# GpSimd adds two shifted score patterns in bf16 for 26 of 160 VectorE key groups of a fused attention and ReGLU kernel

## The chip, the cores and the metric

The kernel runs on one core of a Trainium2 chip. The metric is the device time of one execution, in microseconds. The time before is 677.84 us, the median of three runs (676.66 to 677.92).

Six engines matter here. TensorE multiplies matrices (PE in the profile, with its weight loads shown as PEld), ScalarE (ACT) evaluates exponentials, VectorE (DVE) and GpSimd (POOL) do elementwise work, SyncE (SP) issues most DMAs. Each engine executes its own list of instructions in order, and waits on semaphores that the others raise. [...]

## The reference

With x of 2048 rows and 512 columns, the result is x plus an attention block plus a gated feed-forward block, both fed by the same layer norm. Attention has 32 heads of 16 columns, the feed-forward block 1792 hidden columns:

```python
        scores = jnp.einsum("bhqd,bhkd->bhqk", q, k) * (Dh ** -0.5)
        p = _softmax(scores, axis=-1)
        o = jnp.einsum("bhqk,bhkd->bhqd", p, v)
...
        gate = gate * (lambda x, dt: x.astype(dt))(gate > 0, gate.dtype)
        h = gate * up
        return jnp.einsum("bsf,fd->bsd", h, W_down)
...
    xn = _layernorm(x, axis=-1)
    return x + _A_ref(xn, A_wqkv, A_wo) + _B_ref(xn, B_W_gate, B_W_up, B_W_down)
```

## The kernel before

Attention is the bulk. Its work is cut into 512 key groups: four blocks of 512 queries, four groups of eight heads, the even or the odd four heads of such a group, and sixteen tiles of 128 keys. One key group has four score tiles of 128 keys by 512 queries, one for each head. A score tile is one step of TensorE with four matmuls (`score`, L1584), and half of the array works on it. The softmax needs no maximum here, so a group only needs exp of its scores, and then the product with the values ("pv" steps, `pv_stream`, L1540); a column of ones beside the values gives the sum for the division.

Exponentials are made in two ways:

- 352 groups go to ScalarE. Each is two units (704 in all), and one unit is an exp over 128x1024 scores from PSUM into a slot of `ring` (L1654). Two PSUM slots alternate between units.
- 160 groups go to VectorE and GpSimd (`quad`, L1607; `QUADS` says how many in each of the 32 blocks). VectorE turns each of the four score tiles into 16-bit integers with one add and a clamp at zero (L1615, named d1). Read as bf16, such an integer is a rough exponential: the exponent bits are right, and the fraction is a straight line. To smooth the line, three such patterns are summed: the raw one, and two more that have the integers 31 and 81 added (`SHIFTS`, L433). Before the change GpSimd makes the two shifted patterns from the raw one with a 64-bit integer add over four packed lanes (L1629, named p3, one instruction of 128x2048 16-bit numbers for each pattern). VectorE makes them (L1632) in the first two and the last two groups only. TensorE then does the sum itself: it runs the product with the values once for each of the three patterns, and all of them accumulate in the same PSUM bank. So such a group has six pv steps, two halves of the array for each of the three tensors.

Raw patterns have four buffers (`NRAW`), shifted ones five (`NPAT`). The projections, the gated feed-forward block and the output rows are cut into jobs of a few TensorE steps each and threaded between the units.

GpSimd's instructions come from two sets. `load_library` (L1018) issues one small 64-bit add whose only use is to bring in the set that holds it, with `LIB_NS = 7000` as its cost in the plan. The operations that carry the name "stock", which are the power of the layer norm (L929, a `tensor_tensor`) and the last `iota` (L1667), belong to the other set: the small add is ordered behind those that exist by then, and the iota behind every p3. The kernel has no instruction that loads a set by name.

The order of all instructions was planned beforehand and is written out as a list of operation numbers, `ORDER`, with the buffer numbers in `SLOTS`. `Graph.follow` (L543) replays it: each engine's queue is the list restricted to that engine. It also makes each GpSimd operation that is marked `port` wait for the last VectorE operation so marked before it in the list.

Of the kernel before, what the change touches and what calls it, by code (L numbers as in the profile page):

```python
# [81 lines left out]
POOL_NS = 1014  # L82
LIB_NS = 7000
# [657 lines left out]
def bass_parallel_sum__mha_block__glu_gated_reglu__prompt_kernel(  # L741
# [13 lines left out]
    with ExitStack() as es:  # L755
# [44 lines left out]
        P_b = Pool("b", 4)  # L800
        P_ring = Pool("ring", NRING)
        P_raw = Pool("raw", NRAW)
        P_pat = Pool("pat", NPAT)
        P_qf = Pool("qf", 2)
        P_xn = Pool("xn", 4)
        P_q = Pool("q", NQ)
# [903 lines left out]
```

## Time and profile before

| view | figure |
|---|---|
| median of three runs | 677.84 us |
| profiled execution, its own time | 680.3 us |
| profiled execution, span from first to last instruction | 678.5 us |
| TensorE clock granted, mean | 1.000 |
| GpSimd busy | 334.1 us, 345 instructions |
| ScalarE busy | 659.1 us |
| DMA, mean over the span | 42 GB/s |

The span is shorter than the execution's own time by 1.8 us, which lie around the first and the last instruction. [...] Idle time is put down to what ended it; "issue" stands where the engine waited for nothing that the profile shows.

### The profile page before, as it was taken

Reading aid. Unit: us, or ns where it says so; the run is one execution under the profiler, and the core shown is the slowest. Engines: PE = TensorE matmul, PEld = TensorE weight load, DVE = VectorE, ACT = ScalarE, POOL = GpSimd, SP = SyncE. Lnnn points to the kernel's source line nnn. Section 1 sums busy time; section 2 is a strip of 40 time slices with the busy share of each in tenths; the row PEclk is TensorE's granted clock in tenths of the full one; section 3 lists DMA queues with packets and bytes.
Section 4 is the critical chain, followed back from the end, with each engine's and each line's share of the span. In section 5 each row is a group of like instructions: output and inputs, shape, how many; then the busy total and the mean of one; then the engine's idle time right before and its main releaser. Section 6 shows DMA issues by size and latency. Waiting matters only on the chain.

```text
span 678.5 us, 46119 instructions
## 1 busy us (share of the span) xinstructions
PE 667.7 (98%) x22348; PEld 394.5 (58%) x20912; DVE 594.7 (88%) x1001; ACT 659.1 (97%) x721; POOL 334.1 (49%) x345
## 2 busy tenths in 40 slices
PE   8999999999999999999999999999999999999997
PEld 3455566565565766665665655555565555555663
DVE  8958999998998888999999787999999777889886
ACT  7999999999999999999999999999999999999995
POOL 3201554654546645555556535654546642535650
PEclk9999999999999999999999999999999999999999
DMA  6420111131411121110101110020200012020101
GB/s 195 58 71 13 43 32 27 24 95 40 118 38 28 37 57 29 27 54 19 38 7 26 36 42 22 23 74 4 59 7 19 22 44 72 23 80 15 31 4 43
DMA packets 51478, 28.77 MB, mean 42 GB/s; under 512 B 18840, under 2 KB 50328, under 8 KB 51288
## 3 DMA queue, kind: packets, MB, share of 16 engines
q1 hardware_dynamic: 51144, 25.70, 14.6%
q8 instruction: 169, 2.77, 1.7%
q14 instruction: 21, 0.17, 0.1%
q10 hardware_dynamic: 144, 0.13, 0.1%
HBM read 18.22 MB, written 2.10 MB: 30 GB/s over the span
## 4 chain that ended last, share of the span: by engine, by line
PE 95%; DVE 2%; ACT 1%; issue 1%; DMA 0%; SPq 0%; POOL 0%
PE ps L481 95%; ACT ring L1654 1%; DVE stats L945 0%; DMA x_sb<-in_A_x_dram 0%; DVE xn_sb L968 0%; SPq L858 0%; DVE xnT L1013 0%; DVE o_sb L1410 0%; DVE up_sb L1412 0%; DVE qf L1414 0%; ACT up_sb L937 0%; DVE o_sb L1407 0%; ACT up_sb L936 0%; POOL rstd L943 0%; ACT xn_sb L1429 0%
## 5 line engine op out<-in xcount | busy, mean ns | idle before, releaser
L1654 ACT ACTIVATE ring<-ps 128x1024 bf16<-128x1024 f32 x704 | 651.1, 1085 | 7.4 <-PE ps L481 6.5
L481 PE MATMUL ps<-qT,kT 64*32 64x512 bf16 x8192 | 470.5, 375 | 1.8 <-issue 0.7
L1615 DVE TENSOR_SCALAR qd<-ps 128x512 int16<-128x512 f32 x640 | 418.8, 685 | 53.4 <-PE ps L481 47.3
L1629 POOL INT64_ADD qd<-qd x312 | 321.0, 1043 | 282.0 <-PE ps L481 132.6
L481 PE MATMUL ps<-qd,v_aug 64*32 64x512 bf16 x3840 | 297.1, 375 | 0.5 <-issue 0.4
L1595 PEld LDWEIGHTS <-kT 64*32 64x32 bf16 x8156 | 178.9, 92 | 113.6 <-issue 26.6
L481 PE MATMUL ps<-ring,v_aug 64*32 64x512 bf16 x2816 | 241.6, 375 | 0.4 <-issue 0.2
L1567 PEld LDWEIGHTS <-v_aug 64*32 64x32 bf16 x5256 | 129.5, 92 | 61.2 <-issue 11.8
L481 PE MATMUL ps<-xnT,wgs 64*32 64x512 bf16 x1792 | 136.7, 375 | 0.6 <-issue 0.6
L481 PE MATMUL ps<-xnT,wus 64*32 64x512 bf16 x1792 | 135.9, 375 | 0.0
L481 PE MATMUL ps<-Wd,hT 64*32 64x512 bf16 x768 | 60.9, 375 | 0.0
L1048 PEld LDWEIGHTS <-wus 64*32 64x32 bf16 x1792 | 45.2, 92 | 22.4 <-issue 2.9
L1048 PEld LDWEIGHTS <-wgs 64*32 64x32 bf16 x1792 | 44.2, 92 | 22.4 <-issue 3.5
L1048 PEld LDWEIGHTS <-hT 64*32 64x32 bf16 x1792 | 44.5, 92 | 21.4 <-issue 2.7
L481 PE MATMUL ps<-Wv,hT 64*32 64x512 bf16 x512 | 44.2, 375 | 0.4 <-issue 0.4
L481 PE MATMUL ps<-Wk,hT 64*32 64x512 bf16 x512 | 43.8, 375 | 0.0
L1269 DVE SCALAR_TENSOR_TENSOR hT<-ps,up_sb 128x512 bf16<-128x512 f32 x56 | 38.5, 687 | 5.5 <-PE ps L481 4.8
L1265 DVE COPY up_sb<-ps 128x512 f32<-128x512 f32 x56 | 38.4, 686 | 3.0 <-PE ps L481 2.1
L481 PE MATMUL ps<-Wo_p,x_sb 64*32 64x512 bf16 x480 | 40.5, 375 | 0.1
L481 PE MATMUL ps<-xnT,Wq 64*32 64x512 bf16 x480 | 36.8, 375 | 0.0
L481 PE MATMUL ps<-xnT,Wk 64*32 64x512 bf16 x480 | 35.6, 375 | 0.9 <-DVE xnT L1013 0.8
L481 PE MATMUL ps<-Wv,xnT 64*32 64x512 bf16 x512 | 31.6, 375 | 0.5 <-DVE kT L1106 0.4
(81 smaller groups left out, 219.6 us busy)
## 6 DMA issues: line engine op xcount, KB each, us to landing
wus<-in_B_W_up_dram SPq DMA_DIRECT2D x38, 128.0 KB, 2.9
wgs<-in_B_W_gate_dram SPq DMA_DIRECT2D x38, 128.0 KB, 2.7
xr_sb<-in_A_x_dram SPq DMA_DIRECT2D x16, 128.0 KB, 2.3
qT<-qf SPq DMA_DIRECT2D x120, 16.0 KB, 2.6
o_sb<-o_sb SPq DMA_DIRECT2D x60, 32.0 KB, 2.4
out_dram<-xn_sb SPq DMA_DIRECT2D x15, 128.0 KB, 2.1
x_sb<-in_A_x_dram SPq DMA_DIRECT2D x8, 128.0 KB, 2.8
Wd<-in_B_W_down_dram SPq DMA_DIRECT2D x6, 128.0 KB, 2.8
```

What stands on the lines that cost most here:

```text
L481: return e.add_instruction(mybir.InstMatmult(name=e.bass.get_next_instruction_name(), engine=mybir.EngineType.PE, ins=[e.lower_ap(x), e.lo ...
L1048: e.ldweights(w()[rows, 32 * j:32 * j + 32], tile_position=(rows.start, 32 * j))
L1265: G.op("DVE", 603, lambda e: e.tensor_copy(up_sb[:, tup.slot, :], bank_of(tu)), reads=[tu], writes=[tup], prio=-590)
L1269: G.op("DVE", 603, lambda e: e.scalar_tensor_tensor(out=hT[:, th.slot, :], in0=bank_of(tg), scalar=0.0, in1=up_sb[:, tup.slot, :], op0=ALU ...
L1567: e.ldweights(vs(j), tile_position=(64 * half, 32 * j))
L1595: e.ldweights(ks(m), tile_position=(64 * half, 32 * m))
L1615: G.op("DVE", 601, lambda e, j=j, tx=tx: e.tensor_scalar(qd[:, tq.slot, 512 * j:512 * j + 512], ps[:, BANK[tx.slot], :], IBIAS[3], 0.0, op ...
L1629: G.op("POOL", POOL_NS, lambda e, x=x, n=n: e.int64_add(x().bitcast(I64), raw().bitcast(I64), SHIFTS[n + 1] * LANES), reads=[ti, tq, t_lib ...
L1654: exp_ops[u] = G.op("ACT", ACT_NS, lambda e, tr=tr, k0=k0: e.activation(ring[:, tr.slot, :, :], ps[:, 4 * k0:4 * k0 + 2, :], ACTF.Exp, sca ...
```

## The change

Of the 160 VectorE groups, numbered from 0, every fifth from number 10 to number 135 is treated differently, 26 in all. In such a group GpSimd makes the first shifted pattern as before (p3). Then, for each of the four quarters, it makes the second shifted pattern of that quarter in a small buffer `cuts` (named p5, an integer add of 128x512 16-bit numbers) and adds it in bf16 to the same quarter of the first pattern, in place (named p4, a `tensor_tensor`). There is one buffer `cuts`. TensorE then multiplies two tensors with the values, the raw one and the sum, in four pv steps where there were six. The groups, units, buffers and all constants of the plan stay as they were.

```diff
+ADD_NS = 1130
+CUT_NS = 290
+ADD_PRIO = 3
+ADD_SHARE = 0.2
+ADD_OFF = 0.0
+FIRSTA = 8
+LASTA = 24
...
+        cuts = sb("cuts", [128, 1, 512], I16)
...
+        P_cut = Pool("cut", 1)
...
-                kinds[bk + (t,)] = KINDS[len(kinds) % len(KINDS)]
+                kinds[bk + (t,)] = 3
+        for i, k in enumerate(kinds):
+            if FIRSTA <= i < len(kinds) - LASTA and int(i * ADD_SHARE + ADD_OFF) > int((i - 1) * ADD_SHARE + ADD_OFF):
+                kinds[k] = 2
...
+        def added(key, u, ti, tq, raw, ta, xa):
+
+            G.op("POOL", POOL_NS, lambda e: e.int64_add(xa().bitcast(I64), raw().bitcast(I64), SHIFTS[1] * LANES),
+                 reads=[ti, tq, t_lib], writes=[ta], prio=u, name="p3", port=True)
+            sums = []
+            for j in range(4):
+                cut = slice(512 * j, 512 * j + 512)
+                tc = Tile("cut", P_cut)
+                c = lambda tc=tc: cuts[:, tc.slot, :]
+                G.op("POOL", CUT_NS, lambda e, cut=cut, c=c: e.int64_add(c().bitcast(I64), raw()[:, cut].bitcast(I64), SHIFTS[2] * LANES),
+                     reads=[ti, tq, t_lib], writes=[tc], prio=u + ADD_PRIO, name="p5", port=True)
+                sums.append(G.op("POOL", ADD_NS, lambda e, cut=cut, c=c: e.tensor_tensor(xa()[:, cut].bitcast(BF16), xa()[:, cut].bitcast(BF16), c().bitcast(BF16), ALU.add),
+                                 reads=[ta, tc], prio=u + ADD_PRIO, name="p4", port=True))
+            ta.w += sums
+            for t, x, more in ((ti, raw, [tq]), (ta, xa, [])):
+                pv_stream(key[:3], key[3], [(lambda rows, j=j, x=x: x()[rows, 512 * j:512 * j + 512].bitcast(BF16)) for j in range(4)],
+                          [t] + more, u, u + PV_LAG, "DVE")
...
+            nq[0] += 1
+            if kinds[key] == 2:
+                added(key, u, ti, tq, raw, ta, xa)
+                return prev
             tb, xb = made("qb")
-            nq[0] += 1
...
-        added = [o for o in G.ops if o.name == "p3"]
+        patterns = [o for o in G.ops if o.name in ("p3", "p4")]
...
-        G.op("POOL", LIB_NS, lambda e: e.iota(pid, pattern=[[0, 2]], base=0, channel_multiplier=1), reads=t_masks, writes=[t_pid], prio=NU, order=added + t_rbz.w, name="stock")
+        G.op("POOL", LIB_NS, lambda e: e.iota(pid, pattern=[[0, 2]], base=0, channel_multiplier=1), reads=t_masks, writes=[t_pid], prio=NU, order=patterns + t_rbz.w, name="stock")
```

`ORDER` and `SLOTS` are replaced as a whole: each changed group has 21 operations instead of 16, so the numbers shift, and the list grows from 8030 to 8160 entries. The plan is a fresh one, which the few words with the change call "not searched". The first changed group has the numbers 1206 (p3), then 1207, 1209, 1211, 1213 (p5) and 1208, 1210, 1212, 1214 (p4). Its GpSimd part of the list, with what stands between left out, reads

```
1207 p5, 1208 p4, 1209 p5, 1210 p4, 1260 p3, 1211 p5, 1261 p3, 1212 p4, 1213 p5, 1292 p3, 1214 p4
```

where 1260, 1261 and 1292 are patterns of the groups behind it. All 26 have this form: the p5 and the p4 alternate, and up to two of the other groups' p3 lie between some of them.

More of the change, by code (lines that the diff above doesn't have):

```diff
@@ L92 @@
     91, 92, 101, 102, 112, 115, 94, 103, 118, 113, 95, 340, 341, 116, 119, 104, 96, 122, 117, 342, 120, 343, 105, 344, 121, 98, 123, 100, 345, 124, 365,
[312 rows of a table removed]
[317 rows of a table added]
 ]
 SLOTS = [int(c, 36) for c in (
-    "0001213130200012110232110324115016720118009101a13b210c30210d311ef011012011103220313450108210913670012cd011a0b001e10f001130012110231453080190"
-    "11611703c1d03001a1b001e0f32031110201320030142815008191300611720c112d0001a90241b201021e00f0021312a10112134201312411508321230901261073203c1122"
-    "3db0121ab00030e100f1300211301021c40123101421115300819300216202700312cdd43010a32103b0301e3f002103201001220031e4315003180239026f204313270021c3"
@@ L410 @@
-    "21d0a123b00021e0f2134130211011002201133014101g503011218309231622070112304cd320a1131b0311ehf2030110132130123131021040315024018139020601220071"
-    "i3cd003a0102303b103204e3f0101j30120022310302140351020813920361272030120c1d0131ab042010312ef0130101100131212303402135103040118139011022670121"
-    "c3121d0a2112b01224311e0302f1103311002213302103435008031090020161201344720013cd002130a0b021ef300003513002311232013004124350200118390031162010"
-    "67011c0d0013a0112b031170ef01100431013001213030113423500083110194611071c0311d002a11201b31210121230e21124f02041125011310010118109036111730124c"
@@ L414 @@
-    "13d10311a0103b3032013320e013120f0431005100312310821191403130602137001cd0100142301a303b0210233001e314f0014103125000010120018290016217002c102d"
-    "03010314a2b00212230e21f32040112500011001018001921204300116021003712cd320213a30b00121231021e21340101f1034115300021302120328110961701304031c21"
-    "3d52031ab03123231103300e1113f0401142030503101000301341809301611371420c113d030a1310b012311301e2f130215100411300502010101000811096061120104310"
-    "70c11010d0a2311b7021023200e124021f041226850110021000128301209002611130070140c11d0091a1b3310213131300e0311224f001145c010103001300381901030211"
@@ L418 @@
-    "067010c10dd0a3013b40300012313011231ef001302013450200231214g0318903021000631207032c1d0302a12h1b002321300372e100f403014503000c110d01a10b101200"
-    "11410081103903060170021030010e1012f123004315000304c10d3001a3b1031031001102018394210201617201123031200100e110f011402150010c1d1001a110b0101030"
-    "180110401922161710312220333124e213020f1302405c1d32130a113b0331001208301034020936213702203120302e0120f00013432140520011cd01011330a1103b101100"
-    "031812300190360104730221131003431ef0010101450113103cd01420a310b300501100100213830900326130722312122730e0310f200412005031c001d3192a3b02001031"
@@ L422 @@
-    "014302018a39001604207300222311320111ebf2100401200523c1211d000001210ab0103011041010211820e960122702120133f100e11f0011402402050c012023d0a11gb0"
-    "1030110101080193306h01312047012310103012e31f0i4011305110c10d310013ab010310j423010100118900116700231312132032e11f023112402140050c3112d03a3211"
-    "21b1031200133482013902261003742321300032100e01f202140051202001412c1d00a213b31020810090160730010320203013e1f401411315203101103310c11d1101a000"
-    "12b1012819332013164170321310e011f01411540011210c0311112d021101ab120821012900617230022130032e1314023f001450200001030010c31d20022a1b0081231113"
@@ L426 @@
-    "4900301670300221240303130e11f2104015000103130011c1300003d0a11301b002831090010166750201313001e3104231f04731015300310130c0013d0010a3180b203801"
-    "934032106200317200212130290021e30f0421350020011200c0123401d00a1b420208012009617001123113103e11001f031203134130151010310c16d301431a1b01821291"
-    "026117210202112301e231f1021140015013401010001131c0032d14ab01830911376702130100110123")]
+    "0001213130200012110232110324115061702180101090213a11b0c12d0e13f1030011011022021330314150281190613700c121d0a011b00e1f001310021113024135018019"
@@ new lines @@
+    "0116117030c13d00a11b200e13f0301110210030234018250180119030461102701c102d001a1922b001e201f002013a1201211323014241115038022019310206310272031c"
+    "123d10b2a13b0001e0410f30020111301211c2310241113500813090262310702043c12d03d0a2130b003e0130f02001311020002212300e413010350038129340f261070100"
+    "c12d3001a103b2000e113f320103131010120104330004310g5000181139100361001170023c112d03a1013hb0001e100f0113010110102213243030241050313801390i0062"
+    "13070200c31d0031a1230jb00e1022f00002401013012010330103412530202813009036100734012c0211d002a011b020e10f01000101011000221013201024112351008129"
@@ new lines @@
+    "00206104731002c10d10201a1212b021e1103f0001103010310213301300401050134841009100601017030113c13d500a123b000e1123f30101461100211300014031115073"
+    "800129016112071000c101d00230a1103b0210e01421f02001101102002011132040130510428100930230611702200c103d202a3312b0034e11123f02201333001243125033"
+    "0212013402813900061201071032c100d201a10211b000e411f002010133001140151001101110038211900363117203c0114d3041a0113b01e110f101210310142101502230"
+    "0311100028112090146010070c11100d301a10b102e101f004213030241005013002101002800101902060111027033c110d0301a11023b0204e113f03102111323033415003"
@@ new lines @@
+    "101013028211920306215170c31241d030a1133b0020e01013f021201323000043100503012401002081229100063130703c51d2003a11020b03e10f30000421120330104110"
+    "52030011112000381219200610171000021c160d201a11000b310e00412f00021623070243110250001010102181180920316100127013c4112d0001a102b003e2113f092321"
+    "13433020431250223021003101812019102611c173032c10014d20a102b0032de011f023121133300104210504131001031110g381019120301006300017001033c11d03ah14"
+    "120b0030e11f0327111031034113501301c134d10003012311103a011b0322181390031613171043e110f001211302143103510c011d2010214211000a1210b0801901006101"
@@ new lines @@
+    "07031e01010f03211121033003141353013c411d000010110a1122b01380119026110701110e121f042211130021410250c021d02320133012303a012b100281129020361427"
+    "032e00103f021212330131421115002c1014d2033001013000a01032b202008139100336010070012e13f20330201234040122500013c1d103053011210013a1024b20100811"
+    "90060112700e71200f0002201213024119235030c112d000201110410a1010b01a028122930106112703e1013f00102b132301004133520041c1200d1012011311022a100331"
+    "b00381940103601272023ee2111f022211030343311f35002c11d003000110010g1a1124b00108012091002612070210e1hf1023021143000421153002ci110d201001011101"
@@ new lines @@
+    "2a011b02j1801090100306130704002e132f000221130230032413050302c1131d002401100a130b030048139000613037023e10001f3032121330414101510a1310b203c103"
+    "1d010311431011819100610710120e11f0000121133000410225020a10b20c1200d0101131000483110910036013237003e13f04021103300414050a210b20210c120d002010"
+    "1102081122900136217103e011f00412310330241115301a1130b022c132d23003001113018114390023611170031e123f002201300204311330502a110b02011c10024d0001"
+    "1212101180210902261072306e1510f000201230042174050311a10b000c0102d0382011132108131390103061227401e311f109132021213034213135030a113b0141c13d01"
@@ L431 @@
+    "1031221103381139001601171040e11f002210301302400152200a1132b000c12d6002401210028119200161272011e12313f002211303413520a11b03c4101d010170210810"
+    "90061703e01f0010110123")]
 LOG2E = 1.4426950408889634
```

629 rows, old and new, of the table ORDER are left out of this document.

## The prediction

> **What bounds the kernel now.** I read the page's table of engines first, then the chain of work that ended last, then the costliest groups.
>
> ```profile
> span 678.5 us, 46119 instructions
> ...
> PE 667.7 (98%) x22348; PEld 394.5 (58%) x20912; DVE 594.7 (88%) x1001; ACT 659.1 (97%) x721; POOL 334.1 (49%) x345
> ...
> PE 95%; DVE 2%; ACT 1%; issue 1%; DMA 0%; SPq 0%; POOL 0%
> ...
> L1654 ACT ACTIVATE ring<-ps 128x1024 bf16<-128x1024 f32 x704 | 651.1, 1085 | 7.4 <-PE ps L481 6.5
> ...
> L1629 POOL INT64_ADD qd<-qd x312 | 321.0, 1043 | 282.0 <-PE ps L481 132.6
> L481 PE MATMUL ps<-qd,v_aug 64*32 64x512 bf16 x3840 | 297.1, 375 | 0.5 <-issue 0.4
> ```
>
> TensorE and ScalarE are both full. The chain lies on TensorE for 95% of the span, yet ScalarE's 704 exps occupy 651.1 us and leave it only 7.4 us idle, 6.5 of them behind TensorE. Less TensorE work can therefore bring at most about 7 us, unless the exps shrink too, and they do not. GpSimd is the engine with room: half idle, nothing of it on the chain, and the products that read its patterns (`ps<-qd,v_aug`) stood idle for 0.5 us in all.
>
> Next I cut the span at the first instruction of GpSimd for what will be the first changed group and after the last one for the last changed group, in the windows view, with the rows of the timeline that give the two edges.
>
> ```profile
> 0.00:96.91 96.91, 93.07 (x2858) 51.59 (x2762) 80.25 (x165) 92.11 (x107) 28.98 (x46) 1.00 0.29 72
> 96.91:572.09 475.18, 472.87 (x16072) 286.17 (x14988) 425.23 (x690) 470.41 (x511) 259.82 (x254) 1.00 0.15 39
> 572.09:678.50 106.41, 101.72 (x3446) 56.71 (x3166) 89.25 (x148) 96.60 (x106) 45.34 (x46) 1.00 0.12 31
> ```
> ```profile
> 96.91 2.06 POOL L1629 INT64_ADD qd<-qd  x2 [1.23 <-DVE qd L1615]
> ...
> 567.99 4.10 POOL L1629 INT64_ADD qd<-qd  x4 [8.02 <-DVE x_sb L1534]
> ```
>
> The columns are busy time and count of TensorE, its weight loads, VectorE, ScalarE and GpSimd, then the granted clock (1.00 throughout). The changed groups lie in the middle 475.2 us; 203.3 us lie outside.
>
> **What GpSimd pays when the kind of instruction changes.** This decides the case. These are the rows of GpSimd's groups with shapes, and its timeline at three places.
>
> ```profile
> L929 POOL TENSOR_TENSOR rstd<-vare,expo 128x1 f32<-128x1 f32 x7 | 3.8, 558 | 4.6 <-DVE vare L927 4.6
> L929 POOL TENSOR_TENSOR rstd<-vare,expo 128x4 f32<-128x4 f32 x2 | 2.5, 1230 | 0.2
> L835 POOL MEMSET rb<- 128x512 f32 x2 | 1.1, 528 | 21.6 <-DVE qd L1632 21.6
> L839 POOL CAST identf<-ident 128x128 f32<-128x128 bf16 x1 | 0.3, 293 | 0.0
> L840 POOL CAST selp<-ident 128x4 f32<-128x4 bf16 x1 | 0.2, 189 | 0.0
> L1021 POOL INT64_ADD ints<-ints x1 | 0.2, 183 | 5.4 <-issue 5.4
> L1667 POOL IOTA ints<- 128x2 int32 x1 | 0.1, 129 | 6.9 <-issue 6.9
> ```
> ```profile
> 6.62 0.65 POOL L943 TENSOR_TENSOR rstd<-vare,expo 128x1 f32<-128x1 f32 x1 [0.23 <-DVE vare L939]
> ...
> 26.75 1.41 POOL L929 TENSOR_TENSOR rstd<-vare,expo 128x4 f32<-128x4 f32 x1
> 33.52 0.18 POOL L1021 INT64_ADD ints<-ints  x1 [5.36 <-issue]
> ...
> 63.01 1.04 POOL L1629 INT64_ADD qd<-qd  x1 [7.16 <-DVE qd L1615]
> 64.01 0.29 POOL L839 CAST identf<-ident 128x128 f32<-128x128 bf16 x1
> 67.49 2.06 POOL L1629 INT64_ADD qd<-qd  x2 [3.19 <-DVE qd L1615]
> 69.48 0.53 POOL L835 MEMSET rb<- 128x512 f32 x1
> 69.98 1.04 POOL L1629 INT64_ADD qd<-qd  x1
> ```
> ```profile
> 658.01 2.05 POOL L1629 INT64_ADD qd<-qd  x2 [2.25 <-PE ps L481]
> 667.00 0.13 POOL L1667 IOTA ints<- 128x2 int32 x1 [6.94 <-issue]
> ```
>
> A cast or a memset follows an integer add, and the reverse, with no gap (63.01, 64.01; 69.48, 69.98). But the first integer add behind the `tensor_tensor` of L929 comes 5.36 us late, and the `iota` behind the last integer add 6.94 us late, both with nothing to wait for. I read them as two swaps of GpSimd's instruction set, one in each direction. The code says which operations are on which side: L929's power, a `tensor_tensor`, and the `iota` are named "stock", and the set of the integer adds is loaded only behind the former. The ten `tensor_tensor` of the trace, nine of L929 and the one at 6.62, all run ahead of the first swap (the last of them at 26.75). The new p4 is a `tensor_tensor`, and it stands between integer adds.
>
> [...]
>
> **The change part by part.**
>
> TensorE: 26 groups lose two pv steps of four matmuls each, 208 of 22348. At 667.7 us / 22348 = 29.9 ns a matmul that is 6.2 us; by the middle window, 472.9 us / 16072 = 29.4 ns, it is 6.1. Take 6; at the other end nothing, where ScalarE sets the pace. VectorE and ScalarE keep their instructions, and so does the DMA queue.
>
> GpSimd: each changed group loses one p3 and gains four p5 and four p4. A p3 costs 1.03 us (two in 2.06). The p5 is not in the trace: between 0.18 us (L1021, one word) and 1.04 us (four times the size); on the line between them, 512 numbers being 128 words of 64 bits, 0.18 + 127/511 x 0.86 = 0.39 us; I take 0.40. The p4's work of 512 bf16 is bounded by 0.53 us (a memset of 512, which reads nothing) and 1.23 us (L929's power of four numbers). The casts give (293 - 189) / 124 = 0.84 ns a number; two inputs at that rate, 0.19 + 2 x 0.43 = 1.05 us; take 1.1. So 104 pairs are 104 x 1.5 = 156 us, between 74 and 236.
>
> Swaps: in the order list a p5 stands ahead of each of the 104 p4 and a p3 or p5 behind it, because there is one buffer `cuts`. None of the p4 are neighbours. So each p4 brings one swap in and one out, 208 in all, beside the two of before. One of each is 5.36 + 6.94 = 12.30 us; 104 x 12.30 = 1279 us. If all were as the shorter row, 1115; as the longer, 1444.
>
> Who waits: both pv halves of the sum need all four p4, and TensorE's queue is in order, so everything behind them stands: the next scores, hence ScalarE's next exp and VectorE's next d1. In the order list 8 to 16 exps (mean 10) stand between a group's first p5 and its last p4, 10 x 651.1 / 704 = 9.3 us of planned cover, and one or two more ahead of the first pv of the sum. Seven swaps (43 us) now lie inside that stretch and the eighth behind it, before the next p3.
>
> The sum is bounded by two paths.
>
> Path A, GpSimd alone sets the middle. 286 p3 remain; by the list 16 lie ahead of the first changed group and 40 behind the last p4, so 230 are inside: 237 us. With 1279 + 156 that is 1672 us, and with the 203.3 outside 1875 us.
>
> Path B, no swap hides behind anything and GpSimd's extra arithmetic hides in its idle half: 678.5 + 1279 - 6 = 1952 us.
>
> Which is nearer? When the first pv of the sum blocks TensorE, the list has already given VectorE the d1 of about three further groups (four raw buffers), so GpSimd has p3 work as soon as it returns; and while it swaps back and does them (5.36 + some 5 us), TensorE runs the five to eight us up to the next changed group's d1. GpSimd then hardly waits. I take A and 15 us of waits: a span of 1890, and with the 1.8 us between this execution's span and its own 680.3 us a time of 1892. The median shown, 677.84, is 2.5 us below the profiled execution, which is nothing at this size.
>
> The low end is A with the cheapest of everything, 203 + 1115 + 74 + 237 = 1629, or 1631 as a time. The high end is B with the longer swap, 678.5 + 1444 - 6 = 2116; the dearest p4 and p5 would add up to 236 - 156 = 80 if nothing covered them, of which I take some and stop at 2150.
>
> [...]
>
> **The rivals.**
>
> R1, one direction is cheap: only the return to the integer adds costs, 104 x 5.36 = 557 us. Path A gives 203 + 557 + 156 + 237 = 1153, path B 1230; about 1195. For it: the kernel starts with stock operations and shows no such gap. Against it: the `iota` returns to operations used before, and its row is the longer of the two.
>
> R2, the other side: no swap, because a plain bf16 add of `tensor_tensor` is among the operations that stay, as cast and memset do; only the power would be stock. Then GpSimd has 334 + 156 - 27 = 463 us of work, still under its span, and TensorE's 6 us count as far as ScalarE's idle time in the middle lets them, 475.18 - 470.41 = 4.8 us. The time is 680.3 - 4.8 = 675.5, or 680.3 where nothing of it arrives: not slower. It decides as soon as the first p4 shows no gap. For it: the new operation is not named "stock" in the diff, and cast and memset show that some stay. Against it: the power is the same instruction in the trace, and all its rows lie before the first swap.
>
> R3, no swap, but the sums come late: the last p4 ends 4 x 1.5 = 6.0 us after p3, the plan (1.13 + 0.29 four times) has 5.7, so 26 x 0.3 = 8 us if each delay reaches TensorE: 680.3 - 6 + 8 = 682. For it: the queue of TensorE has only one or two exps between the last p4 and the pv. Against it: GpSimd's waits for TensorE and VectorE now (282 us before its adds) show that it mostly follows them.
>
> **How the numbers follow.** Forecast 0.82, R1 0.05, R2 0.08, R3 0.05. What a measurement tells from no change is 0.2%, 1.4 us. Slower holds the forecast, R1, R3 and a corner of R2: 0.93. Faster is most of R2: 0.05. Same is 0.02. The range 1630 to 2150 is the forecast's own and leaves the rivals out, 0.18.
>
> **What would show it.** Right: 104 `TENSOR_TENSOR` rows in the middle, each 5 to 7 us behind the integer add ahead of it with "issue" as the releaser, the same on the way back, TensorE's busy share near a third with idle time ended by GpSimd, GpSimd on the chain. The p5 and p4 rows give 0.40 and 1.1 us their due. Wrong: p4 rows close behind p5 (R2 or R3, told apart by whether TensorE waits for them), or a gap in one direction only (R1).

## The result and the profile after

The changed kernel takes 2007.26 us (median of three, 2004.21 to 2011.41) where the kernel before takes 677.84: 2.963 times as long, with a 95% interval of 2.954 to 2.973. The forecast was 1892 us, in a range of 1630 to 2150.

The page of the changed kernel, where the span, the table of engines, the granted clock in 40 slices, the chain of work that ended last and the costliest groups are:

```profile
span 2009.4 us, 46690 instructions
...
PE 832.8 (41%) x22140; PEld 432.5 (22%) x21072; DVE 601.8 (30%) x1001; ACT 680.9 (34%) x721; POOL 465.5 (23%) x527
...
PEclk9966766756675676666576566756666675666599
...
issue 58%; PE 21%; POOL 15%; DVE 4%; ACT 0%; DMA 0%; POOLq 0%; DVEq 0%; SPq 0%
...
L1693 ACT ACTIVATE ring<-ps 128x1024 bf16<-128x1024 f32 x704 | 672.9, 1039 | 1316.7 <-PE ps L494 1315.1
L494 PE MATMUL ps<-qd,v_aug 64*32 64x512 bf16 x3632 | 367.6, 452 | 1150.7 <-POOL qd L1668 805.5
```

No engine is full any more, and the one that holds up the rest is the one that looks idlest: GpSimd, busy for 23% of the span. ScalarE stands idle for 1315.1 us behind TensorE, and TensorE's products with the patterns for 1150.7 us: 805.5 of them behind p3 of GpSimd for unchanged groups, and by the view of waits 344.9 behind the bf16 adds (p4). The chain says why a quiet engine can be the bound: 58% of it is "issue", time in which the engine at that link waited for nothing that the profile shows.

GpSimd's groups by shape, with the idle time just before them at the end of each row:

```profile
L1668 POOL INT64_ADD qd<-qd x260 | 268.2, 1037 | 523.8 <-issue 358.3 <-DVE qd L1651 102.7 <-PE ps L494 35.8
L1636 POOL TENSOR_TENSOR qd<-qd,cuts 128x512 bf16<-128x512 bf16 x104 | 118.7, 1141 | 751.5 <-issue 729.8 <-DVE hT L1287 7.5 <-DVE qf L1105 7.2
L1634 POOL INT64_ADD cuts<-qd x104 | 40.6, 390 | 193.6 <-issue 193.6
L1627 POOL INT64_ADD qd<-qd x26 | 27.0, 1037 | 37.3 <-DVE qd L1651 24.4 <-PE ps L494 12.9
```

And its timeline over the first changed group, with the idle time before an instruction in brackets:

```profile
97.72 1.04 POOL L1627 INT64_ADD qd<-qd  x1 [1.40 <-DVE qd L1651]
98.74 0.40 POOL L1634 INT64_ADD cuts<-qd  x1
106.39 1.14 POOL L1636 TENSOR_TENSOR qd<-qd,cuts 128x512 bf16<-128x512 bf16 x1 [7.25 <-issue]
113.34 0.39 POOL L1634 INT64_ADD cuts<-qd  x1 [5.81 <-issue]
120.91 1.14 POOL L1636 TENSOR_TENSOR qd<-qd,cuts 128x512 bf16<-128x512 bf16 x1 [7.18 <-issue]
128.30 1.03 POOL L1668 INT64_ADD qd<-qd  x1 [6.26 <-issue]
129.32 0.39 POOL L1634 INT64_ADD cuts<-qd  x1
129.70 1.03 POOL L1668 INT64_ADD qd<-qd  x1
137.66 1.14 POOL L1636 TENSOR_TENSOR qd<-qd,cuts 128x512 bf16<-128x512 bf16 x1 [6.94 <-issue]
144.60 0.39 POOL L1634 INT64_ADD cuts<-qd  x1 [5.80 <-issue]
144.98 1.03 POOL L1668 INT64_ADD qd<-qd  x1
153.37 1.14 POOL L1636 TENSOR_TENSOR qd<-qd,cuts 128x512 bf16<-128x512 bf16 x1 [7.36 <-issue]
160.32 3.07 POOL L1668 INT64_ADD qd<-qd  x3 [5.82 <-DVE kT L1121]
```

Integer adds follow each other without a gap (128.30, 129.32, 129.70). Around each bf16 add there is one gap of about 7 us and one of about 6. The last row shows how to read a releaser with care: its 5.82 us are put down to VectorE, but it is the return behind a bf16 add and as long as the other returns. By the plan's costs these nine instructions of the group are 1.01 + 4 x 1.42 = 6.7 us; they take 57 (97.72 to 154.51), with three p3 of other groups among them.

The windows view over the middle, from GpSimd's first instruction for a changed group to the first integer add behind the last bf16 add (the columns are as in the prediction), and the row of the timeline that gives the end:

```profile
97.72:1914.28 1816.56, 649.97 (x16284) 326.23 (x15492) 443.49 (x704) 503.48 (x523) 395.02 (x439) 0.65 0.04 10
```
```profile
1914.28 5.16 POOL L1668 INT64_ADD qd<-qd  x5 [5.74 <-PE ps L494]
```

GpSimd is idle for 1816.6 - 395.0 = 1421.6 us there. The way to the bf16 adds takes 751.5 us for 104 of them, 7.23 each. On the way back the rows name "issue" 32 + 60 times in the middle, 193.6 + 358.3 us in all, 6.00 each. The timeline puts the other twelve down to another engine, but they are as long (5.69 to 6.61 us), and all 104 make 624 us. Together 1375.5 us, 13.23 for a pair. Only 46 us of the middle are left as waits for another engine. The granted clock of TensorE, 1.00 in every window before, is 0.65 there.

### The profile page after: what moved, and what is told of

Its sections match the earlier page's. It is cut to its first block, busy times and chain, and to the rows that moved or that the text cites. A ratio compares the mean times of both kernels' runs of the same rounds, so it can differ in the third digit from the quotient of the medians.

```text
span 2009.4 us, 46690 instructions
## 1 busy us (share of the span) xinstructions
PE 832.8 (41%) x22140; PEld 432.5 (22%) x21072; DVE 601.8 (30%) x1001; ACT 680.9 (34%) x721; POOL 465.5 (23%) x527
## 4 chain that ended last, share of the span: by engine, by line
issue 58%; PE 21%; POOL 15%; DVE 4%; ACT 0%; DMA 0%; POOLq 0%; DVEq 0%; SPq 0%
PE ps L494 21%; POOL qd L1668 6%; POOL qd L1636 6%; DVE qd L1651 2%; POOL cuts L1634 2%; POOL qd L1627 1%; ACT ring L1693 0%; DVE stats L960 0%; DVE o_sb L1496 0%; DVE x_sb L1552 0%; DVE xn_sb L1325 0%; DVE up_sb L1283 0%; DVE hT L1287 0%; DVE kT L1121 0%; DVE rb L1549 0%
## 5 line engine op out<-in xcount | busy, mean ns | idle before, releaser
L1693 ACT ACTIVATE ring<-ps 128x1024 bf16<-128x1024 f32 x704 | 672.9, 1039 | 1316.7 <-PE ps L494 1315.1
L494 PE MATMUL ps<-qd,v_aug 64*32 64x512 bf16 x3632 | 367.6, 452 | 1150.7 <-POOL qd L1668 805.5
L494 PE MATMUL ps<-qT,kT 64*32 64x512 bf16 x8192 | 577.2, 439 | 17.7 <-DVE qd L1651 16.0
L1668 POOL INT64_ADD qd<-qd x260 | 268.2, 1037 | 523.8 <-issue 358.3
L1613 PEld LDWEIGHTS <-kT 64*32 64x32 bf16 x8164 | 197.5, 104 | 739.7 <-issue 666.8
L1636 POOL TENSOR_TENSOR qd<-qd,cuts 128x512 bf16<-128x512 bf16 x104 | 118.7, 1141 | 751.5 <-issue 729.8
L494 PE MATMUL ps<-ring,v_aug 64*32 64x512 bf16 x2816 | 281.9, 429 | 0.4 <-ACT ring L1693 0.3
L494 PE MATMUL ps<-xnT,wgs 64*32 64x512 bf16 x1792 | 163.1, 435 | 0.5 <-issue 0.4
L494 PE MATMUL ps<-xnT,wus 64*32 64x512 bf16 x1792 | 160.3, 434 | 0.0
L1634 POOL INT64_ADD cuts<-qd x104 | 40.6, 390 | 193.6 <-issue 193.6
```

What stands on the lines that cost most here:

```text
L494: return e.add_instruction(mybir.InstMatmult(name=e.bass.get_next_instruction_name(), engine=mybir.EngineType.PE, ins=[e.lower_ap(x), e.lo ...
L1613: e.ldweights(ks(m), tile_position=(64 * half, 32 * m))
L1634: G.op("POOL", CUT_NS, lambda e, cut=cut, c=c: e.int64_add(c().bitcast(I64), raw()[:, cut].bitcast(I64), SHIFTS[2] * LANES), reads=[ti, tq ...
L1636: sums.append(G.op("POOL", ADD_NS, lambda e, cut=cut, c=c: e.tensor_tensor(xa()[:, cut].bitcast(BF16), xa()[:, cut].bitcast(BF16), c().bit ...
L1668: G.op("POOL", POOL_NS, lambda e, x=x, n=n: e.int64_add(x().bitcast(I64), raw().bitcast(I64), SHIFTS[n + 1] * LANES), reads=[ti, tq, t_lib ...
L1693: exp_ops[u] = G.op("ACT", ACT_NS, lambda e, tr=tr, k0=k0: e.activation(ring[:, tr.slot, :, :], ps[:, 4 * k0:4 * k0 + 2, :], ACTF.Exp, sca ...
```

## The experiments

What was expected of each kernel stands ahead of its result, and of the code only the lines that matter are shown, with "..." where lines are left out. Times of the kernel before on the same chip were 677.58, 677.20 and 678.08 us in the three batches.

**No swap.** From the changed kernel, the call in each p4 (only the call is shown):

```diff
-e.tensor_tensor(xa()[:, cut].bitcast(BF16), xa()[:, cut].bitcast(BF16), c().bitcast(BF16), ALU.add)
+e.int64_add(xa().bitcast(I64), xa().bitcast(I64), 0)
```

> The changed kernel with its order and all its instructions, but each of the 104 bf16 adds on GpSimd is a 64-bit integer add of zero over 128x2048 numbers (about 1.03 us, against 1.14 for the bf16 add), an operation of the set that is already there. It leaves out the second shifted pattern from the sum. Theory (swaps of the instruction set cost the time): no swaps in the middle, so the time falls by over 1300 us to 672 to 690 us. Rival (the added arithmetic on GpSimd and its late sums cost the time, and the gaps named issue would be there anyway): it stays above 1500 us. Rival (the fresh order is bad in itself): well above 700 us.

Measured: 681.57 us, 1.006 of the time before (1.0035 to 1.0085). The order and the number of instructions are the same. These are its groups by shape:

```profile
L1668 POOL INT64_ADD qd<-qd x260 | 269.0, 1041 | 139.5 <-DVE qd L1651 79.9 <-PE ps L494 46.0 <-DVE x_sb L1552 6.8
L1636 POOL INT64_ADD qd<-qd x104 | 108.2, 1041 | 6.4 <-DVE x_sb L1552 0.8
L1634 POOL INT64_ADD cuts<-qd x104 | 41.5, 400 | 4.6 <-DVE x_sb L1552 1.5
```

The idle time before the 104 sums falls from 751.5 to 6.4 us and the one before the small-buffer adds from 193.6 to 4.6. So the gaps come with the kind of the instruction in the p4: 2007.26 - 681.57 = 1325.7 us, or 6.37 net for each of the 208 swaps. Both rivals named there fall. What GpSimd does inside a gap no run shows; that it brings in the other set is argued from the kernel's `load_library`, and "swap" is this document's name for a gap of 7.23 or 6.00 us.

**The swaps without the adding.** From the changed kernel, again only the call in each p4, two numbers for 512:

```diff
-e.tensor_tensor(xa()[:, cut].bitcast(BF16), xa()[:, cut].bitcast(BF16), c().bitcast(BF16), ALU.add)
+e.tensor_tensor(xa()[:, cut][:, 0:2].bitcast(BF16), xa()[:, cut][:, 0:2].bitcast(BF16), c()[:, 0:2].bitcast(BF16), ALU.add)
```

> The changed kernel, but each of the 104 bf16 adds takes two numbers a partition instead of 512, so nearly all of the second shifted pattern is left out of the sum. 208 swaps as before, the adding nearly gone. Theory (swaps): 2009 less 104 x (1.14 - 0.3), about 1920 us, between 1890 and 1960. Rival (the adding): below 800 us.

Measured, in one run: 1907.11 us. Its row for the bf16 adds:

```profile
L1636 POOL TENSOR_TENSOR qd<-qd,cuts 128x2 bf16<-128x2 bf16 x104 | 19.2, 185 | 749.9 <-issue 714.9 <-DVE qd L1651 34.9
```

An add shrinks from 1141 to 185 ns, 104 of them by 99.4 us; the kernel gets 100.2 us shorter. GpSimd's work counts one for one, so its queue alone sets the pace (path A of the prediction). The idle time before the adds does not shrink with them (749.9 against 751.5 us).

**A quarter of the swaps.** From the kernel before, in its own order: one bf16 add of both patterns for each of the 26 groups, behind the later of the two p3, and no product with the first shifted pattern.

```diff
+if key in marked and t is ta:
+    left_out.update(G.ops[at:at + 2])
...
+G.op("POOL", 1100, lambda e, xa=xa, xb=xb: e.tensor_tensor(xb().bitcast(BF16), xa().bitcast(BF16), xb().bitcast(BF16), ALU.add),
+     reads=[ta, tb], name="sum", port=True)
```

> The kernel before in its own order: both patterns as before, then one bf16 add of 128x2048 on GpSimd for each of the same 26 groups, and TensorE leaves out the product with the first shifted pattern, so the result is that of the change. 52 swaps in the middle instead of 208, the same bf16 adding (26 times about 4.4 us). Theory (swaps): GpSimd alone needs 203 + 252 x 1.03 + 26 x (13.2 + 4.4) = 921 us, with nothing hidden 672 + 458 = 1130 us; about 1000 us. Rival (the adding itself): near 2000 us, as the adding is the same.

Measured, in one run: 1059.17 us. The add takes 4.03 us, with 187.9 us of idle time in front of the 26:

```profile
L1698 POOL TENSOR_TENSOR qd<-qd 128x2048 bf16<-128x2048 bf16 x26 | 104.9, 4034 | 187.9 <-issue 187.9
```

That is 7.23 us again for each swap to the bf16 add. The adding is nearly the same in sum (104.9 against 118.7 us), the swaps are 52 and not 208, and the kernel is 948 us shorter. The rival named there falls. Of the two bounds (921 and 1130 us) the time lies nearer to the upper one than the 1000 us that I said: with one interruption in five groups GpSimd does wait for the others in between (in the whole run 152.4 us for TensorE and 117.1 for VectorE in front of its p3).

**The clock.** The kernel with one sum a group ran at a mean granted clock of 0.838. Its view of waits, for TensorE in front of the sums:

```profile
PE ps L481 <- POOL qd L1698: 236.9, 25, 11.5
```

Into these stops went 36 matmuls of zeros, which add zero to the bank:

```diff
+for _ in range(36):
+    ins = e.matmul(ps[:, BANK[bank.slot], :], nil[:], kT[:, 0, 0:512], start=False, stop=False)
```

> The kernel with one bf16 sum a group on GpSimd (52 swaps, 1059.17 us, mean granted clock 0.838), with 36 more matmuls of zeros (128x128 by 512 columns, some 7.8 us at full clock) in TensorE's queue just ahead of the first product with each sum, where it stands still for 9.5 us on average. They add zero to the bank. Theory (the lower clock after each stop costs time, since here TensorE and not GpSimd alone sets the pace): the clock rises over 0.9 and the time falls to 1000 to 1035 us. Rival (the stops are set by GpSimd, and the clock costs nothing): 1050 to 1070 us with a higher clock.

Measured: 1078.56 us (two runs), with a mean clock of 0.941; the time lies outside both ranges. The row of the products shows that the stops were mostly filled (41.1 us left behind the sum):

```profile
L481 PE MATMUL ps<-qd,v_aug 64*32 64x512 bf16 x3632 | 303.5, 396 | 145.7 <-POOL qd L1640 104.0 <-POOL qd L1699 41.1 <-issue 0.3
```

The clock rose and the kernel got 19 us longer; the gain of 24 us or more that was expected if the clock cost time did not come. But this does not show that the lower clock is free, as the zeros delay what stands behind them. TensorE was busy for 741.1 us with one sum a group; here it was busy for 912.7 us, 201.1 of them with the zeros (7.7 for each 36), so its own work took some 30 us less. Against that, the stops in front of the products were 306.4 us, and stops and zeros together are 145.7 + 201.1 = 346.8 us. What the lower clock costs in the kernel with one sum a group stays open.

**What the change saves on TensorE, alone.** From the kernel before, in its own order, with the two steps of the third product left out in the 26 groups:

```diff
+if t is tb and key in marked:
+    left_out.update(o for o in G.ops[at:at + 2])
```

> The kernel before in its own order, but TensorE leaves out the product with the second shifted pattern in the same 26 groups (the pattern is still made); what the change saves on TensorE, alone. The 6 us of TensorE count only where ScalarE has room, at most 4.8 us of idle time in the middle: 673 to 677 us. Rival (ScalarE and the waits set the pace, the saving is hidden): 677 to 678 us.

Measured: 676.29 us, 0.9985 of the time before (0.9963 to 1.0007): at best 0.4% less, and not told apart from nothing. ScalarE's group in this kernel:

```profile
L1667 ACT ACTIVATE ring<-ps 128x1024 bf16<-128x1024 f32 x704 | 650.0, 1093 | 4.6 <-PE ps L481 4.3
```

Its idle time falls from 7.4 to 4.6 us. A saving of this size is what a full ScalarE leaves room for.

**Late sums or the fresh order.** The kernel without swaps was 0.6% slower than before, though TensorE had less to do. From it, with four numbers a partition in both GpSimd instructions, for 512 in the p5 (shown) and 2048 in the integer add behind it:

```diff
-e.int64_add(c().bitcast(I64), raw()[:, cut].bitcast(I64), SHIFTS[2] * LANES)
+e.int64_add(c()[:, 0:4].bitcast(I64), raw()[:, cut][:, 0:4].bitcast(I64), SHIFTS[2] * LANES)
```

> The changed kernel with its order and no swap, but the 104 integer adds into the small buffer and the 104 adds behind them take four numbers a partition instead of 512, both as integer adds; nearly all of the second shifted pattern is left out of the sum. It takes some 26 x 4 x 1.1 us of GpSimd work out of the kernel in which zero is added as an integer (681.57 us). Theory A (that kernel lost against the one before because its sums come late): 674 to 677 us. Theory B (it lost because of the fresh order): it stays at 680 to 683 us.

Measured: 680.49 us, 1.0052 of the time before (1.0034 to 1.0071). Taking the GpSimd work away changes next to nothing, so late sums are not the loss. What is left is the fresh order, with the 208 short instructions in it; that is concluded by exclusion, and no run shows what in it costs the time. Between this kernel and the one that leaves out the third product in the old order lie 4.2 us, with the same 22140 matmuls. The tables of engines differ in the weight loads, this one's being

```profile
PE 665.6 (98%) x22140; PEld 413.8 (61%) x21072; DVE 590.0 (87%) x1001; ACT 658.0 (97%) x721; POOL 343.9 (51%) x527
```

in the fresh order, and

```profile
PE 664.7 (99%) x22140; PEld 386.2 (57%) x20808; DVE 594.4 (88%) x1001; ACT 658.0 (98%) x721; POOL 333.5 (49%) x345
```

in the old one: 264 loads more in the fresh one. Whether these are the 4 us was not tried.

**The sum on VectorE.** If GpSimd must not change its instructions, VectorE can add. From the kernel before, in its own order:

```diff
+if key in marked and t is ta:
+    left_out.update(G.ops[at:at + 2])
...
+G.op("DVE", 1100, lambda e, xa=xa, xb=xb: e.tensor_tensor(xb().bitcast(BF16), xa().bitcast(BF16), xb().bitcast(BF16), ALU.add),
+     reads=[ta, tb], name="sum", port=True)
```

> The kernel before in its own order: both patterns on GpSimd as before, then VectorE adds the two in bf16 with one instruction of 128x2048 in each of the same 26 groups, and TensorE leaves out the product with the first shifted pattern. The result is that of the change, with no swap. Theory (the swaps were the whole loss, and the saving on TensorE is worth about 1 us, as measured when the third product was left out): the answer hangs on VectorE, which has 475 - 425 = 50 us of idle time in the middle; at 0.7 to 1.2 us an add it loses 18 to 31 of them: 676 to 684 us. Rival (VectorE's delay of the d1 reaches TensorE in full): up to 705 us.

Measured: 719.73 us, 1.065 of the time before (1.061 to 1.069), worse than either bound that I gave. VectorE's group:

```profile
L1698 DVE TENSOR_TENSOR qd<-qd 128x2048 bf16<-128x2048 bf16 x26 | 32.9, 1264 | 18.1 <-POOL qd L1639 18.0
```

There are 32.9 us of adding, 1.26 for each add where I had estimated 0.7 to 1.2, and 18.1 us of waiting for GpSimd in the middle of VectorE's queue. How it reaches the end shows in the group of the exps:

```profile
L1669 ACT ACTIVATE ring<-ps 128x1024 bf16<-128x1024 f32 x704 | 653.2, 1073 | 44.7 <-PE ps L481 44.0
```

ScalarE's idle time grows from 7.4 to 44.7 us, 37 of the 42.5 us that the kernel got longer. So the same instruction was moved back in that queue, half way to the first product that needs it:

```diff
...
+vec = [n for n in range(at, stop) if G.ops[order[n]].eng == "DVE"]
+at = vec[len(vec) // 2] + 1 if vec else at
```

> The kernel in which VectorE adds the two patterns (719.73 us), with that instruction moved back in VectorE's queue to half way between the patterns and the first product that needs the sum; nothing else changes. In the earlier place VectorE stood idle for 18.0 us in front of the 26 adds, waiting for GpSimd. Theory A (the wait of VectorE's queue is part of the loss): the 18 us mostly go, 698 to 708 us, and not below 26 x 1.26 = 33 us over 676. Theory B (the adds alone hold up the d1, wherever they stand): 715 to 722 us. In no case under 690 us.

Measured: 699.70 us, 1.032 of the time before (1.028 to 1.036). The same group in that kernel:

```profile
L1698 DVE TENSOR_TENSOR qd<-qd 128x2048 bf16<-128x2048 bf16 x26 | 32.5, 1250 | 1.8 <-POOL qd L1639 1.7
```

The wait is gone and 20 us with it. The 32.5 us of adding stay, and the kernel is still 21.6 us longer than before. TensorE's rows show stops of about that size:

```profile
L481 PE MATMUL ps<-qT,kT 64*32 64x512 bf16 x8192 | 472.2, 375 | 9.2 <-DVE qd L1625 8.0
L481 PE MATMUL ps<-qd,v_aug 64*32 64x512 bf16 x3632 | 283.5, 375 | 14.4 <-DVE qd L1698 14.1
```

The products now wait for the sums themselves (14.1 us), and the scores for VectorE's d1 (8.0 us); the kernel before has next to nothing of either (0.5 us of idle time in front of the products, 1.8 in front of the scores). Against the earlier place, by the views of waits, TensorE's wait for the d1 fell from 23.6 to 8.0 us and the one for the sums grew from 6.8 to 14.1. No version that beats the kernel before was found, and a saving on TensorE that could not be told apart from nothing leaves little to look for.

## Why the prediction was right

The mechanism, the count and the bound were right: two swaps for each p4, both with a price (7.23 and 6.00 us), paid in GpSimd's queue, and everything else behind it. The size was low by 119 us of span (1890 against 2009.4). By its own terms, with what they measured:

| term | predicted us | measured us |
|---|---|---|
| 208 swaps | 1279 | 1375 |
| 104 p5 and 104 p4 | 156 | 40.6 + 118.7 = 159 |
| waits of GpSimd in the middle | 15 | 46 |
| p3 in the middle | 237 | 395.0 - 159.3 = 236 |
| outside the middle | 203 | 2009.4 - 1816.6 = 193 |

The step that was mis-sized is the price of a swap. I took one row for each direction, 6.94 and 5.36 us, as if they were means. Over 104 of each they are 7.23 (6.68 to 8.15) and 6.00 (5.69 to 6.61). The other kernels keep the two swaps of before, one to the small add at the start and one to the `iota` at the end. In the kernel without the third product the view of waits has them as

```profile
POOL ints L1680 <- issue: 7.9, 1, 7.9
...
POOL ints L1030 <- issue: 5.3, 1, 5.3
```

Over nine of the kernels, all but the one with the shorter integer adds, the swap to the `iota` takes 6.8 to 7.9 us, so that the row of 6.94 is one draw among others. The one to the small add takes 5.2 to 5.6 us in the six kernels in the old order and 5.9 to 6.2 in three in the fresh one. The row of 5.36 lies below the shortest of the 104 returns, and so does its like in each kernel in the old order: it was not a bad draw of the same thing, and why the first swap is shorter there stays open.

The part on who waits was right in that TensorE stands and everything behind it with it, but named the wrong releaser for most of it. It had the products with the sum standing for the p4, which is 344.9 us of the 1150.7; 805.5 end with a p3 of an unchanged group, which stood among the swaps. Path A counts GpSimd alone and does not hang on this; only the 15 us of waits do, and they measured 46.

The choice of path A over path B was right for 208 swaps: the shorter adds show it one for one. For 52 swaps it is not, which the kernel with one sum a group shows; there the truth lay between the paths.

The prices from neighbouring rows held: 0.40 us for the p5 (0.39), 1.1 us for the p4 (1.14).

The cap on TensorE's saving was in the right place, but 4.8 us was too much: it measured 1.3 us in time (677.58 - 676.29, not told apart from nothing) and 2.8 us in ScalarE's idle time. It drowned in the rest here; in R2 it would have been the whole answer, and too large. Without swaps, with an integer add in the place of the bf16 add, the fresh order does not reach R2's 675.5 us: it takes 681.57. That is R3's size (682) by luck, since R3's mechanism, late sums, was ruled out by the shorter integer adds.

R1 is out, since both directions have their price.

The sum has no term for TensorE's clock. In the first changed group TensorE stands for 23.84 us up to 129.39 us, and in the windows view the granted clock is 1.00 up to 107 us, 0.50 from 108 to 134 and 1.00 again from 136 to 138. I take it that this lower clock adds little where GpSimd sets the pace, as GpSimd waits for all others in the middle for 46 us only; no run tests that by itself.

## What to carry to other kernels

GpSimd was busy for half of the span before, and yet there was no room in it for 104 instructions of another kind, each with 13.23 us of gaps around it. A busy share alone does not tell this: look in the trace for gaps with no releaser around a change of kind, count how often the new code would alternate, and multiply. Where alternating can't be avoided, do all work of one kind in a row; here a fourth of the swaps, with nearly the same adding, took 948 us less. And before trading work to a second engine, measure what the saving on the first is worth by leaving the work out.

## What was not expected

The price of the swap to the bf16 add did not depend on the add behind it: 749.9 / 104 = 7.21 us ahead of adds of two numbers, 187.9 / 26 = 7.23 ahead of adds of 2048. Twenty-six adds of 1.25 us on VectorE, which has 50 us of idle time in the middle before the change, cost 22 us even when VectorE hardly waited in front of them (1.8 us): then TensorE waited for VectorE.
